# Messages kept in PSUM and taken at the start of a period

## The chip, the cores and the metric

The kernel runs on one core of a Trainium2 chip. The metric is device time in microseconds; three runs of the kernel before gave 9139.07, 9145.55 and 9146.39 us, median 9145.55.

## The reference

A message-passing layer on a graph of 12,500 nodes with 800,000 edges; D = 64, edge attributes of 16 numbers, all in fp32:

```python
N, deg, D, De = 12500, 64, 64, 16
E = N * deg
m_in = jnp.concatenate([x[src], x[dst], e_attr], axis=-1)
msg = _silu(m_in @ w_msg)                 # E x D
agg = _segment_sum(msg, dst, N)           # N x D
return _silu(jnp.concatenate([x, agg], axis=-1) @ w_upd)
```

## The kernel before

The nodes are cut into 128 buckets of 98. The product of `w_msg` is split by its rows: `A_d` holds `x @ w_msg[0:64]` for all nodes in HBM, `BW` holds for each bucket the 98 rows `x @ w_msg[64:128]` with the 16 rows for `e_attr` below them, so that one product with a one-hot of the local destination and the edge's attributes gives the rest of a message. The kernel does two things side by side, in software-pipelined *periods* written out by hand (`period`): it sorts edges into buckets, and it computes messages of edges that are sorted already.

**Sorting** (class `Step`, 1024 edges a step, 782 steps). ScalarE makes one-hots of the buckets (`onehot`: eight squares and a Relu, tile `hf`); VectorE sums them up (`sums`, tile `G`); TensorE counts (`count`, tile `z`); VectorE takes ranks (`ranks`, L418) and expands the records into slots (`expand`, tile `X`, L431); TensorE moves them to their buckets (`move`, tile `pl`, L447); ScalarE copies a chunk out (`blk`, L451) and GpSimd scatters it to the store `st` in HBM. The four stages of a step lie in successive periods. A step holds 8 tiles of 128 edges; a chunk holds 8 tiles in the first 140 steps and 12 later, so there the widths of the expansions, and of the matmuls one period behind them, go round with period three.

**Messages** (class `Batch`, 8 tiles of 128 edges, 6 in one stage). In its first period GpSimd gathers the rows of `A_d` by source index (`gather`, L629, one indirect DMA a tile, tile `g`, three buffers) and VectorE makes the one-hot `q` (L634). In the second, TensorE transposes it (`tq`), ScalarE copies it to `qt` (L646), and TensorE takes the product with the bucket's `BW` into the PSUM bank `pre` (`product`, L652). In the third, `message` adds the gathered rows to `pre` on VectorE (L658), the sum going to SBUF, and ScalarE takes the Silu (L659). Where tiles of a bucket come in units of four (`QU`), `parts` splits the fp32 message into three bf16 pieces: it reads the upper halves of the fp32 words as bf16 and subtracts, two VectorE instructions (L667). These batches are called split; all but the first stage's and the last ones are. In the fourth period TensorE reduces the pieces with the one-hot into the PSUM bank `ag` (`reduce`, L678; L680 where not split), and VectorE adds the sums to the accumulators (`add`, L691 and L693). At the end the nodes are updated from the accumulators.

**Groups.** A `Group` of 64 tiles is formed ahead of its use: `fourth` and `middle` compute from the buckets' pointers which tiles are taken. TensorE puts sums into a tile `ps` (`middle`), which VectorE reads one period later, in `fourth`: L535 and L536 in one period, L574 and L575 (`rows`) in the next. `ps` has the tag "ag", and the pool `pag` has one buffer, so `ps` and the aggregate `ag` of `reduce` use one bank in turn. The framework makes the first write of a new tile wait for all reads of the tile that had the buffer before it, wherever in the text they stand.

Every engine works through its own instructions in the order in which `period` calls the functions; semaphores come from the data. Before the change the order on VectorE is: one-hot `q`, reading of a forming group, ranks, message sum, addition of the aggregate, expansion, sums of the one-hots, placing of a chunk, two subtractions. On ScalarE: the next step's one-hot, copy of attributes, weights, copy of the transposes, Silu, copies for sums and chunks. On TensorE: count, transposes, reduction, moves, product (between the moves in every third period), sums of a forming group.

Of the kernel before, what the change touches and what calls it, by code (L numbers as in the profile page):

```python
# [14 lines left out]
P = 128  # L15
NBK = 128
BK = 98
D = 64
# [12 lines left out]
BT = 8  # L31
NBG = 8
GT = NBG * BT
QU = 4
# [12 lines left out]
def mpnn_kernel(tc, x, e_attr, src, dst, w_msg, w_upd, out):  # L47
    nc = tc.nc
# [22 lines left out]
    with es:  # L71
# [90 lines left out]
        class Nodes:  # L162
# [193 lines left out]
        mp = pool("mp", 2)  # L356
# [245 lines left out]
        class Batch:  # L602
# [50 lines left out]

            def message(t):
                w = t.n * D
                t.msg = mp.tile([P, 3, BT * D], F32, name="msg")
                u_ = t.msg[:, 2, :]
                nc.vector.tensor_tensor(out=u_[:, 0:w], in0=t.pre[:, 0:w], in1=t.g.rearrange("p a b -> p (a b)")[:, 0:w], op=OP.add)  # L658
                nc.scalar.activation(t.msg[:, 0, 0:w], u_[:, 0:w], AF.Silu)  # L659

            def parts(t):

                t.split = t.grp.u == QU
                if t.split:
                    up = t.msg.bitcast(BF16).rearrange("p k (f two) -> p k f two", two=2)
                    for k in range(2):
                        nc.vector.tensor_tensor(out=t.msg[:, k + 1, :], in0=t.msg[:, k, :], in1=up[:, k, :, 1], op=OP.subtract)  # L667

            def reduce(t):
                t.ag = pag.tile([P, 512], F32, name="ag")  # L670
                w = 3 * D
                if t.split:
                    q = t.q.bitcast(BF16).rearrange("p i (k two) -> p i k two", two=2)[:, :, 0:BK, 1]
                    m = t.msg.bitcast(BF16).rearrange("p k (f two) -> p k f two", two=2)[:, :, :, 1]
                for i in range(t.n):
                    u, k = i // t.grp.u, i % t.grp.u
                    if t.split:
                        nc.tensor.matmul(t.ag[0:BK, u * w:(u + 1) * w].rearrange("p (k d) -> p k d", d=D), q[:, i, :], m[:, :, i * D:(i + 1) * D], start=(k == 0), stop=(k == t.grp.u - 1))  # L678
                    else:
                        nc.tensor.matmul(t.ag[0:BK, u * D:(u + 1) * D], t.q[:, i, 0:BK], t.msg[:, 0, i * D:(i + 1) * D], start=(k == 0), stop=(k == t.grp.u - 1))  # L680

            def add(t):
                if t.b0 is not None:
# [14 lines left out]
        def period(step=None, batch=None, ptr_new=None):  # L698

            h, z, p, s = step, pipe["h"], pipe["z"], pipe["s"]  # L700
            q, t, a, r = batch, pipe["q"], pipe["t"], pipe["a"]
# [6 lines left out]
                s.scatter()  # L708
            if q:
                q.gather(BT // 2, BT)  # L710
            if h:
                h.onehot()
            if q:
                q.onehot()
            for g in forms:
                g.fourth()
            if z:
                z.count()
            if t:
# [2 lines left out]
                t.transpose(1)  # L722
            if r:
                r.reduce()
            if z:
                z.ranks()
            if a:
                a.message()
            if r:
                r.add()  # L730
            if z:
                z.expand()
            if h:
                h.sums()
            if p:
# [179 lines left out]
        while work["used"] < large or (work["forming"] and work["forming"][-1].k < 2):  # L915
            b = take()
# [67 lines left out]
        while work["used"] < whole or lasts or work["cur"] is not None or work["forming"]:  # L984
            b = take()
# [165 lines left out]
```

## Time and profile before

| what | value |
|---|---|
| median of three runs | 9145.55 us |
| the profiled execution's own time | 9133.99 us |
| its span, first to last instruction | 9132.2 us |
| busy: PE, PE weight loads, DVE, ACT, POOL | 8125.5, 5898.7, 8140.8, 5100.7, 6771.0 us |
| mean granted TensorE clock | 0.966 |

Busy times say how long an engine had instructions in execution. POOL's row counts only the descriptor work of its DMAs; the 0.30 us of issue between two of them is shown as idle. A row of the timeline gives start, busy time, engine, line, operation, tiles, shapes and count, and in brackets the idle time before and what ended it. A row of the groups gives busy time, mean ns of one, and idle time before.

### The profile page before, as it was taken

To read this page: it belongs to the slowest core of one execution; us is meant where nothing else is said; L and a number is where in the kernel's file an instruction comes from. 1 tells how busy PE (TensorE), PEld (TensorE's weight loads), DVE (VectorE), ACT (ScalarE), POOL (GpSimd) and SP (SyncE) were. 2 spreads that over 40 slices of the span, in tenths; PEclk is the share of its full clock that TensorE was granted. 3 is DMA by queue.
4 is the path that set the end of the run, shared out by engine and by line. 5 is a ranking of instruction groups with operands and counts; after the bars stand their busy time and mean duration, and the time that the engine had idled before them with its cause. 6 is when DMAs were issued, how large, how long until landed. Compare 5 with 4: busy or idle time off the path is not lost. (4 is left out here: it accounts for less than half of the span.)

```text
span 9132.2 us, 146484 instructions
## 1 busy us (share of the span) xinstructions
PE 8125.5 (89%) x44080; PEld 5898.7 (65%) x44842; DVE 8140.8 (89%) x17569; ACT 5100.7 (56%) x12609; POOL 6771.0 (74%) x6915
## 2 busy tenths in 40 slices
PE   8999999988888888898889898898888888888677
PEld 5677776666666666666666666666666666666676
DVE  7899999999999999999999999999999999998332
ACT  6566665555555555555555555555555555555222
POOL 1677777777777777777777777777777777777776
PEclk9999999999999999999999999999999999999666
DMA  2222222222222222222222222222222222222323
GB/s 66 55 60 62 61 60 56 50 56 50 55 54 50 55 51 55 49 56 51 55 50 54 56 51 50 54 55 50 56 51 54 50 55 55 51 54 48 58 48 50
DMA packets 650600, 492.47 MB, mean 54 GB/s; under 512 B 482887, under 2 KB 519303, under 8 KB 649799
## 3 DMA queue, kind: packets, MB, share of 16 engines
q0 software_dynamic: 238976, 349.72, 16.9%
q1 hardware_dynamic: 408119, 132.58, 6.9%
q8 instruction: 360, 5.90, 0.3%
q14 instruction: 441, 3.61, 0.1%
q10 hardware_dynamic: 2704, 0.66, 0.1%
HBM read 330.05 MB, written 152.30 MB: 53 GB/s over the span
## 5 line engine op out<-in xcount | busy, mean ns | idle before, releaser
L629 POOL DMA_INDIRECT g<-A_d,sidx x6322 | 6186.0, 978 | 1953.4 <-issue 1557.3
L447 PE MATMUL pl<-X,hf 128*128 128x223 f32 (+5 forms) x12512 | 4093.2, 478 | 0.0
L447 PEld LDWEIGHTS pl<-X,hf 128*128 128x128 f32 x12512 | 2303.0, 191 | 1263.5 <-issue 912.4
L431 DVE TENSOR_TENSOR X<-cb,rec 128x442 f32<-128x442 f32 (+5 forms) x3128 | 2647.3, 909 | 27.1
L383 ACT ACTIVATE hf<-iof,shi 128x128 f32<-128x128 f32 x6256 | 1909.4, 389 | 1056.7 <-PE pl L447 1053.2
L652 PEld LDWEIGHTS pre<-w,qt 114*128 114x128 f32 x10496 | 1289.8, 195 | 322.3 <-issue 298.5
L652 PE MATMUL pre<-w,qt 114*128 114x64 f32 x10496 | 1265.2, 275 | 44.3 <-DVE msg L658 39.9
L659 ACT ACTIVATE msg<-msg 128x512 f32<-128x512 f32 (+1 forms) x818 | 501.8, 613 | 1270.3 <-DVE msg L658 1265.5
L418 DVE TENSOR_REDUCE rank<-z 128x8 f32<-128x1024 f32 x782 | 949.6, 1214 | 66.5 <-PE z L413 64.6
L658 DVE TENSOR_TENSOR msg<-pre,g 128x512 f32<-128x512 f32 (+1 forms) x818 | 546.2, 668 | 485.7 <-DMA g<-A_d,sidx 285.5
L646 ACT ACTIVATE qt<-tq 114x1024 f32<-114x1024 f32 (+1 forms) x818 | 800.8, 979 | 312.2 <-PE tq L643 308.9
L411 PE MATMUL z<-G,onesb 128*128 128x384 bf16 x1564 | 515.8, 330 | 467.3 <-DVE G L392 416.4
L451 ACT ACTIVATE blk<-pl 128x512 f32<-128x512 f32 (+1 forms) x568 | 325.2, 573 | 1074.9 <-PE pl L447 1034.6
L667 DVE TENSOR_TENSOR msg<-msg 128x512 f32<-128x512 f32 x1312 | 903.6, 689 | 22.9
L384 ACT ACTIVATE hf<-hf,ones 128x1024 f32<-128x1024 f32 x782 | 899.1, 1150 | 25.4
L643 PE MATMUL tq<-ident,q 128*114 128x128 f32 x6322 | 887.1, 286 | 14.2 <-ACT nodes L188 12.8
L643 PEld LDWEIGHTS tq<-ident,q 128*114 128x114 f32 x6322 | 781.9, 142 | 139.8 <-ACT nodes L188 20.5
L678 PE MATMUL ag<-msg,q 128*98 128x192 bf16 x5248 | 580.0, 253 | 307.9 <-DVE rb L575 118.2
L469 POOL DMA_INDIRECT st<-blk,ptrs x567 | 566.7, 999 | 333.4 <-issue 147.8
L634 DVE TENSOR_TENSOR q<-cb,lo 128x784 f32<-128x784 f32 (+1 forms) x818 | 768.5, 939 | 0.7
L678 PEld LDWEIGHTS <-q 128*98 128x98 bf16 x5248 | 497.1, 126 | 396.6 <-issue 338.1
L411 PEld LDWEIGHTS <-onesb 128*128 128x128 bf16 x1564 | 152.7, 98 | 384.6 <-DVE G L392 281.1
(145 smaller groups left out, 6768.0 us busy)
## 6 DMA issues: line engine op xcount, KB each, us to landing
g<-A_d,sidx POOLq DMA_INDIRECT x6322
ea<-in_e_attr SPq DMA_DIRECT2D x260, 192.0 KB
rt<-st SPq DMA_DIRECT2D x1312, 34.0 KB
st<-blk,ptrs POOLq DMA_INDIRECT x567
rt<-st SPq DMA_DIRECT2D x434, 8.5 KB
nodes<-in_x SPq DMA_DIRECT2D x62, 98.0 KB
rt<-st SPq DMA_DIRECT2D x320, 17.0 KB
A_d<-nodes SPq DMA_DIRECT2D x32, 98.0 KB
```

Source lines behind the costliest of these rows:

```text
L383: nc.scalar.activation(c.hf[:, k, :], iof, AF.Square, bias=c.hi[:, k:k + 1])
L384: nc.scalar.activation(c.hf, c.hf, AF.Relu, bias=ones, scale=-1.0)
L418: nc.vector.tensor_reduce(out=c.rank, in_=c.z, axis=AX.X, op=OP.max)
L431: nc.vector.tensor_tensor(out=c.x[:, k:k + 2, 2:2 + n * R].rearrange("p k (s c) -> p k s c", c=R), in0=hit[:, k:k + 2, 0:n, None].to_broad ...
L447: nc.tensor.matmul(pl[:, 0:w], c.hf[:, k, :], c.x[:, k, 0:w], start=False, stop=(n == c.size - 1))
L629: nc.gpsimd.indirect_dma_start(out=t.g[:, i, :], out_offset=None, in_=A_d, in_offset=bass.IndirectOffsetOnAxis(ap=t.grp.sidx[:, k:k + 1], ...
L634: nc.vector.tensor_tensor(out=t.q[:, 0:n, 0:BK], in0=ioB[:, None, 0:BK].to_broadcast([P, n, BK]), in1=t.grp.lo[:, i0:i0 + n, None].to_broa ...
L643: nc.tensor.transpose(t.tq[0:KQ, j * P:(j + 1) * P], t.q[:, j, :], ident)
L646: nc.scalar.activation(t.qt[:, 0:w], t.tq[0:KQ, 0:w], AF.Copy)
L652: nc.tensor.matmul(t.pre[:, i * D:(i + 1) * D], t.qt[:, i * P:(i + 1) * P], w, start=True, stop=True)
L667: nc.vector.tensor_tensor(out=t.msg[:, k + 1, :], in0=t.msg[:, k, :], in1=up[:, k, :, 1], op=OP.subtract)
L678: nc.tensor.matmul(t.ag[0:BK, u * w:(u + 1) * w].rearrange("p (k d) -> p k d", d=D), q[:, i, :], m[:, :, i * D:(i + 1) * D], start=(k == 0 ...
```

## The change

The message sum is written back to `pre` in PSUM. In split batches the Silu works there in place, ScalarE rounds it to bf16 with a copy into a bf16 tile, VectorE subtracts that piece from `pre` in place, ScalarE rounds the rest, and VectorE subtracts once more into the third piece. In other batches the Silu goes from PSUM to an fp32 tile. In the period, the message sum becomes VectorE's first instruction and Silu and first rounding ScalarE's first; the first subtraction stands behind the one-hot `q`, the second behind the ranks. The next step's one-hot on ScalarE moves behind the copy of the transposes. The reading of a forming group (`fourth`) moves from ahead of the ranks to behind the second subtraction, and in the text behind `reduce`; the addition of the aggregate moves behind the expansion.

```diff
             def message(t):
                 w = t.n * D
-                t.msg = mp.tile([P, 3, BT * D], F32, name="msg")
-                u_ = t.msg[:, 2, :]
-                nc.vector.tensor_tensor(out=u_[:, 0:w], in0=t.pre[:, 0:w], in1=t.g.rearrange("p a b -> p (a b)")[:, 0:w], op=OP.add)
-                nc.scalar.activation(t.msg[:, 0, 0:w], u_[:, 0:w], AF.Silu)
-
-            def parts(t):
-
                 t.split = t.grp.u == QU
+                pre = t.pre[:, 0:w]
+                nc.vector.tensor_tensor(out=pre, in0=pre, in1=t.g.rearrange("p a b -> p (a b)")[:, 0:w], op=OP.add)
                 if t.split:
-                    up = t.msg.bitcast(BF16).rearrange("p k (f two) -> p k f two", two=2)
-                    for k in range(2):
-                        nc.vector.tensor_tensor(out=t.msg[:, k + 1, :], in0=t.msg[:, k, :], in1=up[:, k, :, 1], op=OP.subtract)
+                    t.msg = mp.tile([P, 3, BT * D], BF16, name="msg")
+                    nc.scalar.activation(pre, pre, AF.Silu)
+                    nc.scalar.activation(t.msg[:, 0, 0:w], pre, AF.Copy)
+                else:
+                    t.msg = mp.tile([P, BT * D], F32, name="m32")
+                    nc.scalar.activation(t.msg[:, 0:w], pre, AF.Silu)
+
+            def part(t, k):
+
+                if t.split:
+                    nc.vector.tensor_tensor(out=t.pre if k == 1 else t.msg[:, k, :], in0=t.pre, in1=t.msg[:, k - 1, :], op=OP.subtract)
+                    if k == 1:
+                        nc.scalar.activation(t.msg[:, k, :], t.pre, AF.Copy)
...
-            if h:
-                h.onehot()
+            if a:
+                a.message()
             if q:
                 q.onehot()
-            for g in forms:
-                g.fourth()
+            if a:
+                a.part(1)
             if z:
                 z.count()
...
             if r:
                 r.reduce()
+            if h:
+                h.onehot()
             if z:
                 z.ranks()
             if a:
-                a.message()
+                a.part(2)
+            for g in forms:
+                g.fourth()
+            if z:
+                z.expand()
             if r:
                 r.add()
-            if z:
-                z.expand()
...
-            if a:
-                a.parts()
             for g in forms:
                 g.middle()
```

More of the change, by code (lines that the diff above doesn't have):

```diff
@@ L677, in reduce @@
                     if t.split:
-                        nc.tensor.matmul(t.ag[0:BK, u * w:(u + 1) * w].rearrange("p (k d) -> p k d", d=D), q[:, i, :], m[:, :, i * D:(i + 1) * D], start=(k == 0), stop=(k == t.grp.u - 1))
+                        nc.tensor.matmul(t.ag[0:BK, u * w:(u + 1) * w].rearrange("p (k d) -> p k d", d=D), q[:, i, :], t.msg[:, :, i * D:(i + 1) * D], start=(k == 0), stop=(k == t.grp.u - 1))
                     else:
-                        nc.tensor.matmul(t.ag[0:BK, u * D:(u + 1) * D], t.q[:, i, 0:BK], t.msg[:, 0, i * D:(i + 1) * D], start=(k == 0), stop=(k == t.grp.u - 1))
+                        nc.tensor.matmul(t.ag[0:BK, u * D:(u + 1) * D], t.q[:, i, 0:BK], t.msg[:, i * D:(i + 1) * D], start=(k == 0), stop=(k == t.grp.u - 1))
             def add(t):
```

1 line of the change is left out of this document (removed).

## The prediction

> **What bounds the kernel now.** I read the page first, then the busy time by stages, then the groups and the waits of the even middle (2000 to 8000 us), and last the timeline of single periods.
>
> ```profile
> span 9132.2 us, 146484 instructions
> 500.00:1000.00 500.00, 495.18 (x2949) 382.71 (x3004) 473.80 (x1250) 321.92 (x805) 379.03 (x395) 1.00 0.27 62
> 4000.00:5000.00 1000.00, 896.17 (x4814) 632.65 (x4901) 943.79 (x1961) 574.96 (x1428) 763.54 (x777) 0.99 0.24 53
> 8600.00:8800.00 200.00, 155.91 (x878) 146.19 (x878) 73.22 (x217) 51.49 (x106) 151.66 (x161) 0.61 0.32 54
> ```
>
> The columns of a stage are its length and the busy time of PE, PE weight loads, DVE, ACT and POOL. There are three stages. Early (until about 1344 us, batches that are not split) PE is full: 495 of 500 us. In the middle (to about 8400 us) DVE is at 94% and POOL at 76%. At the end only POOL keeps its pace. The middle holds three quarters of the time, so I look for what it waits for.
>
> ```profile
> L629 POOL DMA_INDIRECT g<-A_d,sidx x4290 | 4226.4, 985 | 1307.3 <-issue 1046.1 <-DMA g<-A_d,sidx 174.0 <-DVE q L634 33.8
> L667 DVE TENSOR_TENSOR msg<-msg 128x512 f32<-128x512 f32 x1072 | 738.2, 689 | 18.6
> L418 DVE TENSOR_REDUCE rank<-z 128x8 f32<-128x1024 f32 x536 | 650.2, 1213 | 0.0
> L678 PE MATMUL ag<-msg,q 128*98 128x192 bf16 x4288 | 467.6, 251 | 257.0 <-DVE rb L575 97.4 <-DVE msg L667 96.4 <-DVE wl L536 61.1
> L658 DVE TENSOR_TENSOR msg<-pre,g 128x512 f32<-128x512 f32 x536 | 368.2, 687 | 173.7 <-issue 84.8 <-DMA g<-A_d,sidx 84.5
> L659 ACT ACTIVATE msg<-msg 128x512 f32<-128x512 f32 x536 | 337.3, 629 | 944.8 <-DVE msg L658 944.4
> L451 ACT ACTIVATE blk<-pl 128x512 f32<-128x512 f32 x358 | 211.9, 592 | 567.8 <-PE pl L447 567.8
> ```
>
> ```profile
> DVE msg L658 <- issue: 84.8, 126, 1.8
> DVE msg L658 <- DMA g<-A_d,sidx: 84.5, 122, 2.5
> ```
>
> The L418 row counts 536 periods in 6000 us, 11.19 us each. POOL never rests in them: 985 ns of gather and about 0.30 us of issue, over and over. DVE has one stall, ahead of the message sum (L658): 173.7 us, in 126 + 122 = 248 waits. DVE instructions that do not wait start about 0.08 us before the one ahead ends, so a wait costs that as well: 173.7 + 248 x 0.08 = 194 us, or 0.36 us per period. So the gathers set the pace, and DVE by itself would need 11.19 - 0.36 = 10.83 us. DVE and POOL are nearly even, and whichever the change makes longer decides.
>
> One period in which a forming group is read back shows the rest:
>
> ```profile
> 5777.99 1.41 DVE L667 TENSOR_TENSOR msg<-msg 128x512 f32<-128x512 f32 x2
> 5779.32 0.97 DVE L634 TENSOR_TENSOR q<-cb,lo 128x784 f32<-128x784 f32 x1
> 5780.20 0.15 DVE L574 SCALAR_TENSOR_TENSOR row<-ps,iof 1x16 int32<-1x16 f32 x1
> 5780.29 0.15 DVE L575 CAST rb<-ps 1x16 int32<-1x16 f32 x1
> 5780.37 1.20 DVE L418 TENSOR_REDUCE rank<-z 128x8 f32<-128x1024 f32 x1
> 5780.50 0.85 PE L678 MATMUL ag<-msg,q 128*98 128x192 bf16 x8 [1.50 <-DVE rb L575]
> 5780.92 1.00 ACT L646 ACTIVATE qt<-tq 114x1024 f32<-114x1024 f32 x1
> 5781.18 6.03 PE L447 MATMUL pl<-X,hf 128*128 128x359 f32 x16
> 5781.78 0.69 DVE L658 TENSOR_TENSOR msg<-pre,g 128x512 f32<-128x512 f32 x1 [0.21 <-DMA g<-A_d,sidx]
> 5782.39 0.55 DVE L691 TENSOR_REDUCE sum<-ag 98x128 f32<-98x384 f32 x1
> 5782.51 0.63 ACT L659 ACTIVATE msg<-msg 128x512 f32<-128x512 f32 x1 [0.59 <-DVE msg L658]
> 5783.37 0.17 DVE L427 TENSOR_TENSOR X<-rank,limc 128x8 f32<-128x8 f32 x1
> 5786.82 0.45 DVE L392 TENSOR_TENSOR G<-hf 128x256 bf16<-128x256 f32 x1
> 5787.05 1.90 PE L652 MATMUL pre<-w,qt 114*128 114x64 f32 x16
> 5787.75 2.44 ACT L383 ACTIVATE hf<-iof,shi 128x128 f32<-128x128 f32 x8
> 5788.30 1.41 DVE L667 TENSOR_TENSOR msg<-msg 128x512 f32<-128x512 f32 x2
> 5790.21 1.15 ACT L384 ACTIVATE hf<-hf,ones 128x1024 f32<-128x1024 f32 x1
> ```
>
> The product (L652), whose result the next message sum needs, ends at 5788.95, after the two roundings (L667) of 5788.30 have begun. That is harmless today, because the message sum comes 3.8 us behind the period's first L667.
>
> **Part 1, a new wait on DVE in every split period.** Call m the start of the message sum, now the first DVE instruction of a period. Behind it comes the one-hot (L634), 0.61 us later (5781.78 to 5782.39 is how long a message sum holds DVE). The first subtraction would follow 0.89 us after that (5779.32 to 5780.20 plus rounding), at m + 1.49. But it now needs two ScalarE instructions, the Silu and the first rounding, one after the other. ACT starts 0.04 us after the sum's end (5782.47 to 5782.51). Neither a Silu on PSUM nor a rounding copy is in the trace. The nearest rows are the Silu in SBUF, 629 ns, and the copy out of PSUM of the same shape, 592 ns. For the rounding I take 592, for the Silu 600, as it reads PSUM like the copy, with 550 to 630 as bounds; 0.03 us for each handover. So it starts at m + 0.69 + 0.03 + 0.60 + 0.03 + 0.59 + 0.03 = m + 1.97, and DVE stands still for 0.48 us. Queued behind it on DVE are ranks, expansion and everything else. The second rounding copy (0.59) is hidden by ranks (1.13 us, 5780.37 to about 5781.5, if nothing is waited for). One thing is saved: today the second L667 waits for the first and the pair takes 1.33 us (5777.99 to 5779.32); apart they take 2 x 0.61. Net +0.48 - 0.11 = +0.37 us per period.
>
> **Part 2, the operands move to PSUM.** In the trace a tensor_tensor with a PSUM input takes 687 ns (L658), one with both in SBUF 689 (L667), so I cost this at nothing for DVE. The Trainium skill (VectorE: DVE Perf Modes, section "The TRN2 errata") gives 120 cycles fixed for PSUM-sourced and 58 for SBUF-sourced VectorE instructions; by that, at the page's 0.96 GHz, two subtractions would be dearer by 0.13 us per period, an estimate of +82 us in all. The two rows here show no such difference.
>
> For POOL the move counts:
>
> ```profile
> 5778.88 1.34 POOL L629 DMA_INDIRECT g<-A_d,sidx  x1 [0.30 <-issue]
> 5781.77 0.94 POOL L629 DMA_INDIRECT g<-A_d,sidx  x1 [0.30 <-issue]
> ```
>
> The instructions of L536, one for each group that forms, from 500 to 1344 us and from 1344 to 8400 us:
>
> ```profile
> L536 DVE TENSOR_SCALAR wl<-ps x24: 146/146/150, 504.1 to 1316.0; 128x1 f32<-128x1 f32 x24
> L536 DVE TENSOR_SCALAR wl<-ps x79: 146/148/151, 1378.8 to 8383.6; 128x1 f32<-128x1 f32 x79
> ```
>
> Beside the L667 pair a gather takes 1.34 us, beside the message sum 0.94. The mean of 985 ns holds (985 - 944) x 4290 = 176 us of such stretching, 0.33 us per period; most of it goes, and POOL would need about 10.9 us. DVE then needs 10.83 + 0.37 = 11.20 us and becomes the bound: the gather waits go (-0.36), the new wait comes (+0.37). A group of 64 tiles makes 8 batches and 79 groups fall into the middle, so 632 periods: -228 + 234 = +6 us.
>
> **Part 3, the reading of a forming group moves behind the second subtraction.** The group's sums ("ps") and the aggregate ("ag") share one PSUM bank, a pool with one buffer. So PE's reduction (L678) must wait until DVE has read the sums: L536 in one period of a group, L575 in the next. Today it waits for that too (1.50 us in the quoted period), but the reading stands right behind the one-hot. After the change it stands behind message, one-hot, subtraction, ranks, subtraction: m + 1.97 + 0.61 + 1.13 + 0.61 = m + 4.32, done at m + 4.56, and L678 starts at m + 4.61. In the quoted period, with m = 5777.99, that is 5782.60 and not 5780.50: 2.10 us later. Queued behind L678 on PE are the 16 matmuls of L447 and the product, so the product ends at 5788.95 + 2.10 = 5791.05. DVE alone would be ready for the next message sum at 5782.48 (reading done) + 4.93 (L427 to the next L667) + 0.98 (the addition, L691 to L427) = 5788.39. It now waits for the product: 2.7 us, and as DVE is the bound, all of it is lost. In the groups whose second reading falls in such a period (short expansion, long L447 matmuls; I count 44 of 79 by following L574 through the timeline) that costs 44 x 2.7 = 119 us. In the other 35 the product comes early in the second period and PE is late into the period after it. I have no single row for that: bounds are 0 and 2.7 per group, I take the middle, 1.4, or 49 us. Together +168 us.
>
> **Part 4, the early stage.**
>
> ```profile
> 768.53 1.45 PE L652 MATMUL pre<-BW,qt 114*128 x12
> 769.66 0.76 DVE L634 TENSOR_TENSOR q<-cb,lo 128x588 f32<-128x588 f32 x1
> 771.47 1.00 PE L680 MATMUL ag<-msg,q 128*98 128x64 f32 x10
> 772.15 0.55 DVE L658 TENSOR_TENSOR msg<-pre,g 128x384 f32<-128x384 f32 x1
> ```
>
> PE runs without a gap here and the reduction (L680) starts 1.49 us after the product's end (769.98). With the message sum first, DVE starts it at 770.03, then one-hot (770.50), ranks (771.18), reading (772.31), read at 772.53: L680 would start at about 772.58 in a reading period, 1.1 us later. 24 groups have 48 such periods, PE is the bound, so +53 us; bounds are 0 and, with one more microsecond of ranks, 100.
>
> **Part 5, what is hidden.** The one-hot of the next step moves behind the transposes' copy on ACT. Its squares and Relu (2.44 + 1.15, about 3.5 us with overlap) then follow copy (until m + 3.29), weights and the 1.00 us of L646 and end at about m + 8.0. DVE needs them at L392, which in the quoted period would come at m + 4.49 + 3.45 + 0.98 = m + 8.9. Margin 0.9 us: hidden, and if that cover fails, each 0.1 us of lateness is 63 us. At the end POOL sets the pace and no length changes, but with DVE as the bound POOL may enter that stage with up to two batches more done (16 x 1.25 = 20 us): I take -10.
>
> **The sum.** +6 + 168 + 53 - 10 = +217 us on the profiled execution, which took 9134.0 us (1.8 more than its span); the median of the three runs, 9145.55, is 11.6 above that. On the median: 9360 us, +2.4%. The measurement of this kernel can tell a difference of about 0.2% (18 us).
>
> **The rivals.** *A, the gathers win: faster.* If what bounds is the gather queue and the roundings cost DVE little, the period falls to POOL's 10.9 us, 0.3 x 632 = about -190, so near 8955 us, or 9010 with the early loss. The Trainium skill (SBUF — State Buffer, section "Who interferes with whom") says that a VectorE instruction with two SBUF inputs contends with a GpSimd instruction that reads SBUF, and one with a single SBUF input does not; the 1.34 and 0.94 us rows agree. For it: the stretched gathers. Against it: DVE would have to come out below 10.9 us, so the new stall would have to be under about 0.18 us and not 0.48, and the readings would have to be hidden. Chance 0.08. *B, the bank costs nothing: about the same.* If the readings' lateness is absorbed, +6 - 10 and some of the early loss are left: 9140 to 9190, say 9155. For it: PE has 10% idle time in the middle. Against it: in the quoted period nothing idle stands between the reduction's start and the product's end (5780.50, 5781.18, 5787.05, 5788.95). Chance 0.12. *C, tighter coupling in ordinary periods too: slower still.* The message sum now meets the product's end, and ACT's chain of 8.0 us meets the sums' start, in every period. At 0.3 us per period: +190 more, 9550. For it: in the quoted period the product ends after the period's end even now. Against: the new stall of 0.48 delays DVE, not PE, which widens that margin. Chance 0.08.
>
> **How the numbers follow.** The forecast has 0.72, with its own range from 9290 (35 groups at nothing, short Silu) to 9450 (all groups at 2.7, early loss 100). Leaving out A and part of C, and taking in most of B, the range is 9160 to 9450. Faster: A and a sliver of B, 0.10. Same: 0.05, the part of B near 9146. Slower: 0.85.
>
> **What would show it.** Right: the first subtraction waits for ACT by 0.4 to 0.5 us in every split period; the gather waits at the message sum vanish, and in their place stand waits for the product of over 2 us, some 44 of them; gathers mean under 0.96 us; L678 waits for L536 and L575 by about 3 us. Wrong: POOL still without pause in the middle (A), no product waits (B), L392 waiting for L384 (C).

## The result, and the profile after

The changed kernel takes 9648.03 us (median of four runs, 9644.43 to 9651.14) against 9142.36 us for the kernel before on the same chip: ratio 1.0554, 95% interval 1.0538 to 1.0570. The direction was forecast (slower, 0.85), the size was not: +506 us where the sum gave +217, outside the range (9450).

The page's first line:

```profile
span 9646.1 us, 147735 instructions
```

The three stretches that were shown of before, with the same columns (length; busy PE, weight loads, DVE, ACT, POOL; granted clock; DMA share; GB/s):

```profile
500.00:1000.00 500.00, 463.53 (x2672) 353.62 (x2723) 430.94 (x1141) 305.45 (x732) 344.16 (x355) 0.98 0.21 55
4000.00:5000.00 1000.00, 884.43 (x4561) 621.72 (x4645) 895.88 (x1838) 650.97 (x1520) 705.12 (x734) 0.95 0.19 50
8600.00:8800.00 200.00, 176.62 (x904) 123.51 (x920) 180.00 (x368) 130.69 (x305) 140.99 (x147) 0.95 0.19 49
```

No engine is full any more: PE falls from 495 to 464 of 500 us in the early stage, DVE from 944 to 896 and POOL from 764 to 705 of 1000 us in the middle (the last row now still lies in the middle). The granted TensorE clock falls from 0.99 to 0.95. Set side by side by the first split addition and the last ranks, the early stage ends 113 us later (1348 to 1461), the 633 periods of the middle take 7495 us instead of 7071 (11.84 a period against 11.17), and the rest is 24 us shorter: +514 us of span.

Groups of the middle (2000 to 8000 us): busy time, mean ns of one, and idle time before with what ended it.

```profile
L629 POOL DMA_INDIRECT g<-A_d,sidx x4049 | 3871.8, 956 | 1237.7 <-issue 1038.8 <-DMA g<-A_d,sidx 115.0 <-DVE cb L428 39.6
L447 PE MATMUL pl<-X,hf 128*128 128x359 f32 (+5 forms) x8101 | 2956.5, 519 | 0.0
L682 PE MATMUL ag<-msg,q 128*98 128x192 bf16 x4056 | 431.8, 251 | 293.7 <-DVE wl L536 173.0 <-DVE rb L575 120.7
L670 DVE TENSOR_TENSOR pre<-pre,msg 128x512 f32<-128x512 f32 x506 | 354.1, 700 | 204.6 <-ACT msg L662 204.6
L658 DVE TENSOR_TENSOR pre<-pre,g 128x512 f32<-128x512 f32 x506 | 354.0, 700 | 167.2 <-PE pre L652 135.7 <-issue 14.3 <-DMA st<-blk,ptrs 3.7
L469 POOL DMA_INDIRECT st<-blk,ptrs x337 | 344.7, 1023 | 546.9 <-ACT blk L451 509.3 <-issue 37.6
L662 ACT ACTIVATE msg<-pre 128x512 bf16<-128x512 f32 x506 | 302.3, 597 | 15.9
L444 PE MATMUL pl<-done,onesb 1*128 1x512 bf16 x337 | 135.4, 402 | 229.3 <-ACT blk L451 229.3
L464 DVE SCALAR_TENSOR_TENSOR LOST<-blk 128x1 f32<-128x1 f32 x337 | 52.1, 155 | 102.4 <-ACT blk L451 101.7
```

The forecast wait is there: L670 stands 0.40 us for the first rounding (L662) in each of 506 periods, 0.48 with the lost overlap. The gathers are down to 956 ns, and their waits ahead of the message (L658) are gone, but the message now waits for the product. Three rows were not forecast: the first matmul of a new chunk (L444), the placing of a chunk (L464) and the scatter (L469) all wait for the chunk's copy `blk` on ScalarE.

A period in which a forming group is read; only some of its rows are shown:

```profile
5029.33 0.70 DVE L658 TENSOR_TENSOR pre<-pre,g 128x512 f32<-128x512 f32 x1 [0.18 <-issue]
5031.30 0.70 DVE L670 TENSOR_TENSOR pre<-pre,msg 128x512 f32<-128x512 f32 x1 [0.40 <-ACT msg L662]
...
5033.04 0.68 DVE L670 TENSOR_TENSOR msg<-pre,msg 128x512 bf16<-128x512 f32 x1
5033.71 0.15 DVE L536 TENSOR_SCALAR wl<-ps 128x1 f32<-128x1 f32 x1
5033.90 1.44 PE L682 MATMUL ag<-msg,q 128*98 128x192 bf16 x8 [3.54 <-DVE wl L536]
5035.81 6.84 PE L447 MATMUL pl<-X,hf 128*128 128x223 f32 x16
5042.49 1.90 PE L652 MATMUL pre<-w,qt 114*128 114x64 f32 x16
5044.42 0.70 DVE L658 TENSOR_TENSOR pre<-pre,g 128x512 f32<-128x512 f32 x1 [3.44 <-PE pre L652]
```

Two stretches of the same period, for TensorE alone (length, PE busy, granted clock):

```profile
5031.00:5035.00 4.00, 1.09 (x8) 0.82 0.15 34
5035.00:5039.00 4.00, 4.00 (x12) 0.50 0.11 25
```

TensorE stands 3.54 us for the reading, then runs reduction, moves and product, and VectorE stands 3.44 us for the product: 15.1 us from message to message. The stretches show its clock: 0.82 in the one with the pause, 0.50 in the next.

Every period of the middle can be sorted by what it does, from one batch's one-hot to the next (474 ordinary ones; 79 that read `ps` for L536, "first"; 79 that read it for L575, "second"). Mean length in us:

| kernel | ordinary | first reading | second reading |
|---|---|---|---|
| before | 11.04 | 11.84 | 11.28 |
| after | 11.51 | 12.80 | 12.92 |

So the middle's +425 us are 474 x 0.47 = 223 in ordinary periods and 79 x (0.96 + 1.64) = 206 in reading periods. In the early stage the 59 reading periods are longer by 1.82 (30) and 1.76 us (29), which is 106 of its 113 us.

### The profile page after: what moved, and what is told of

It reads as the page before. It is cut to its first block, busy times and chain, and to the rows that moved or that the text cites. A ratio compares the mean times of both kernels' runs of the same rounds, so it can differ in the third digit from the quotient of the medians.

```text
span 9646.1 us, 147735 instructions
## 1 busy us (share of the span) xinstructions
PE 8445.0 (88%) x44080; PEld 6090.6 (63%) x44842; DVE 8179.4 (85%) x17569; ACT 5947.6 (62%) x13921; POOL 6638.8 (69%) x6915
## 5 line engine op out<-in xcount | busy, mean ns | idle before, releaser
L629 POOL DMA_INDIRECT g<-A_d,sidx x6322 | 6045.0, 956 | 2045.1 <-issue 1624.7
L447 PE MATMUL pl<-X,hf 128*128 128x223 f32 (+5 forms) x12512 | 4413.1, 507 | 0.0
L447 PEld LDWEIGHTS pl<-X,hf 128*128 128x128 f32 x12512 | 2478.8, 205 | 1674.8 <-issue 1277.2
L661 ACT ACTIVATE pre<-pre 128x512 f32<-128x512 f32 x656 | 381.9, 582 | 1787.6 <-DVE pre L658 1787.6
L469 POOL DMA_INDIRECT st<-blk,ptrs x567 | 575.8, 1015 | 889.5 <-ACT blk L451 672.0
L658 DVE TENSOR_TENSOR pre<-pre,g 128x512 f32<-128x512 f32 (+1 forms) x818 | 557.5, 682 | 446.5 <-PE pre L652 200.4
L384 ACT ACTIVATE hf<-hf,ones 128x1024 f32<-128x1024 f32 x782 | 898.2, 1149 | 25.4
L670 DVE TENSOR_TENSOR pre<-pre,msg 128x512 f32<-128x512 f32 x656 | 459.0, 700 | 277.0 <-ACT msg L662 276.5
L672 ACT ACTIVATE msg<-pre 128x512 bf16<-128x512 f32 x656 | 391.8, 597 | 372.3 <-DVE pre L670 372.3
```

What stands on the lines that cost most here:

```text
L384: nc.scalar.activation(c.hf, c.hf, AF.Relu, bias=ones, scale=-1.0)
L447: nc.tensor.matmul(pl[:, 0:w], c.hf[:, k, :], c.x[:, k, 0:w], start=False, stop=(n == c.size - 1))
L469: i = nc.gpsimd.indirect_dma_start(out=st, out_offset=bass.IndirectOffsetOnAxis(ap=c.ptr, axis=0), in_=c.blk[:, 2:], in_offset=None)
L629: nc.gpsimd.indirect_dma_start(out=t.g[:, i, :], out_offset=None, in_=A_d, in_offset=bass.IndirectOffsetOnAxis(ap=t.grp.sidx[:, k:k + 1], ...
```

## The experiments

All times are medians; the ratio is to the kernel before on the same chip.

| run | what it is | us | ratio, 95% interval |
|---|---|---|---|
| a1 | after, reading early | 9383.17 | 1.0265 (1.0247 to 1.0282) |
| a2 | after, one-hot first | 10180.63 | 1.1136 (1.1118 to 1.1155) |
| a3 | both | 9327.47 | 1.0203 (1.0186 to 1.0220) |
| a5 | after, TensorE kept at work (transposes into a new buffer) | 10032.15 | 1.0973 (1.0955 to 1.0992) |
| a6 | after, the same into the bank `ag` | 9896.85 | 1.0838 (1.0820 to 1.0856) |
| a7 | a1, twelve of them into the bank `ag` | 9542.02 | 1.0448 (1.0431 to 1.0465) |
| a9 | a1, the twelve into the tile `tq` | 9185.37 | 1.0062 (1.0045 to 1.0079) |
| a10 | after, the twelve into `tq`, sixteen into the bank `ag` | 9638.15 | 1.0560 (1.0542 to 1.0577) |
| b1 | after's data, before's order | 9255.36 | 1.0137 (1.0120 to 1.0154) |
| b2 | before, reading late | 9274.99 | 1.0158 (1.0141 to 1.0175) |
| b4 | before, message first | 9149.51 | 1.0021 (1.0011 to 1.0031) |
| c4 | a1, ranks ahead of the subtraction | 9128.49 | 1.0000 (0.9990 to 1.0009) |
| c5 | c4, second subtraction later | 9023.16 | 0.9885 (0.9868 to 0.9901) |
| c6 | c5, early message in its old place | 8989.89 | 0.9849 (0.9833 to 0.9866) |

### Undoing the two moves: a1, a2, a3

```diff
 a1:             if q:
                     q.onehot()
+                for g in forms:
+                    g.fourth()
                 if a:
                     a.part(1)
 a2:        +    if h:
+                    h.onehot()
                 if a:
                     a.message()
```

> The changed kernel with the reading of the forming group (fourth) put back right behind the batch's one-hot, ahead of reduce. Three theories for the +506 us. READING: fourth behind reduce holds the one bank ag, TensorE stands 2 to 3.5 us in each reading period (127 waits of ag in 6,000 us, against 105 waits of pl for the chunk copy), and this is most of the loss: its share by count of waits is 127 of 232 of the middle's +425 us, 233 us, and half to all of the early stage's +113; so about 9300 to 9360 us, the waits of ag for wl and rb gone. CHUNK COPY: the copy of pl queued on ScalarE behind the moved one-hot is the loss: 9580 us or more, waits of ag gone and nothing won. COUPLING: the message first, with ScalarE between its sum and its first subtraction, costs by itself: 9600 us or more.

> The changed kernel with only the step's one-hot (eight Squares and a Relu on ScalarE) put back to the front of the period, ahead of the message. CHUNK COPY: the waits of pl and of LOST for the copy go, 105 of 232 waits of the middle, so 190 us of its +425, less up to 150 us for a Silu that stands behind the one-hot (ScalarE waited 3.4 us before a Silu in the one period looked at, and the one-hot takes 3.6): 9460 to 9610 us. READING: 9640 us or more, since the bank is held as before. COUPLING: later than 9650, by the longer wait of the first subtraction (0.3 us in each of 762 periods, some 9800).

> The changed kernel with both moved back: the reading ahead of reduce, the step's one-hot at the front. READING and CHUNK COPY together: the two savings add, 9648 - 300 - 190 + 150 = about 9150 to 9310 us, near the kernel before, and TensorE has hardly a pause over 2 us and few stretches at half clock. COUPLING: 9550 us or more; what is left above 9142 then belongs to the message-first order.

Measured: a1 wins 265 us, 23 us short of READING's range (9300 to 9360) and far from the other two: the waits of `ag` fall to 28 us. a2 lies far above CHUNK COPY's range and above the 9800 of COUPLING, and separates no two theories: TensorE's waits for the chunk's copy go, but with the late reading kept, the one-hot in front is 530 us worse than after. Its Squares wait for a buffer that the late moves free, the Silu stands behind them, and the first subtraction waits up to 5.5 us for it (577 us in 6,000). a3 is 56 us better than a1, and misses its 9150 to 9310 by 17 us. Groups of a1:

```profile
L682 PE MATMUL ag<-msg,q 128*98 128x192 bf16 x4160 | 428.6, 246 | 28.1 <-DVE wl L536 14.5 <-DVE rb L575 13.4
L658 DVE TENSOR_TENSOR pre<-pre,g 128x512 f32<-128x512 f32 x520 | 363.7, 699 | 130.6 <-PE pre L652 91.9 <-issue 15.6 <-DMA st<-blk,ptrs 4.6
L447 PE MATMUL pl<-X,hf 128*128 128x461 f32 (+5 forms) x8312 | 2998.6, 515 | 0.0
L444 PE MATMUL pl<-done,onesb 1*128 1x512 bf16 x346 | 140.2, 405 | 349.4 <-ACT blk L451 349.4
L464 DVE SCALAR_TENSOR_TENSOR LOST<-blk 128x1 f32<-128x1 f32 x346 | 53.5, 155 | 64.2 <-ACT blk L451 64.0
```

Rows of a1's timeline, where a chunk closes and the next opens:

```profile
5020.85 1.90 PE L652 MATMUL pre<-w,qt 114*128 114x64 f32 x16
5022.63 1.15 ACT L384 ACTIVATE hf<-hf,ones 128x1024 f32<-128x1024 f32 x1
5024.14 0.58 ACT L451 ACTIVATE blk<-pl 128x512 f32<-128x512 f32 x1
5024.77 0.58 PE L444 MATMUL pl<-done,onesb 1*128 1x512 bf16 x1 [2.02 <-ACT blk L451]
5025.28 3.79 PE L447 MATMUL pl<-X,hf 128*128 128x223 f32 x8
```

With the reading out of the way, the second cause stands alone. In every third period a chunk closes ahead of the product and the next opens behind it. The copy `blk` now queues on ScalarE behind the moved one-hot (its Relu, L384, ends at 5023.78, and one short copy stands between), TensorE pauses 2.02 us, and the eight matmuls behind the pause take 3.79 us. The same eight behind a pause of 0.47 us in the kernel after:

```profile
5015.85 2.00 PE L447 MATMUL pl<-X,hf 128*128 128x223 f32 x8
```

In the kernel before, the first matmul of a chunk waits for nothing. Its group in the middle:

```profile
L444 PE MATMUL pl<-done,onesb 1*128 1x512 bf16 x357 | 137.5, 385 | 0.0
```

a3 shows that the moved one-hot makes this pause. Over all such places between 2000 and 8000 us, the next chunk opens straight behind the product in the kernel before and in a3, and 2.02 us behind it in a1 (means); the eight matmuls that follow take 2.00, 2.01 and 3.24 us. With the pause, VectorE's waits for the copy (64.0 us in a1, 0.9 in a3) and for the product (91.9 and 1.9) go too. What a3 gains by this it loses in part at the first subtraction: with the Silu behind the one-hot on ScalarE, its wait grows from 144.0 to 263.9 us.

### Is it the pause or the clock behind it: a5, a6, a7, then a9, a10

TensorE repeats transposes of the batch where it stood, so that it stays at work; nothing is moved. a5 writes them to a new buffer of the pool of `tq`, a6 and a7 to free columns of the bank `ag`, a9 and a10 the twelve to `tq` itself and a10 the sixteen to free columns of `ps`. (a5 repeats sixteen at both places; the lines below are those of the other four, with the tile written to left out where it is not `ps`.)

```diff
+            for g in forms:
+                if t and g.b0 is None and g.k in (1, 2):
+                    t.warm(16, g.ps)      # a6, a10: ahead of reduce
             if r:
                 r.reduce()
 ...
+            if t and r and p and p.turn == 1:
+                t.warm(12)                # a7, a9: this one alone
             if p:
                 p.move(1)
```

> The changed kernel in its own order; in periods in which a forming group reads, and in those in which a chunk opens behind the product, TensorE repeats the batch's eight transposes twice into the other buffer of that tile (about 2.1 us at full clock), so that it works where it stood. Nothing else is moved; the repeated values are not used. CLOCK: the pauses cost mostly by the half clock that follows (809 us at half rate in the middle, 217 stretches of 3.4 us): the stretches fall below 60, TensorE gets back up to 1.7 us for each, and the time to 9300 to 9450 us. PAUSE: the wait itself is what is lost, or VectorE sets the pace whatever the clock: 9640 to 9750 us, though the stretches at half clock go.

> The changed kernel in its own order, with transposes of the batch repeated on TensorE into columns of the bank ag that nobody reads: 16 (2.1 us) ahead of reduce in the periods in which a forming group's answer is read, 12 (1.6 us) ahead of the second move in the periods in which a chunk opens behind the product. It replaces a5, whose repeated transposes had to wait for ScalarE's copy of the one tile they share with tq. Nothing is moved; the repeated values are not used. CLOCK: the half clock behind the pauses lengthens the later products of the same period, so that the message and LOST wait: TensorE's product of the chunks falls from 5.68 back to 5.25 us a period, the stretches at half clock from 217 in the middle to below 60, and the time to about 9400 to 9500 us (up to 0.25 us in each of 633 periods and half of the early stage's 72 us). PAUSE: what is lost is the waiting itself, and VectorE's waits stay at 1.25 us a period: 9620 us or more, though the half clock goes.

> a1 (reading early) with the 12 repeated transposes ahead of the second move in the periods in which a chunk opens behind the product; there TensorE stood 173 times for 2.0 us in a1 and ran 208 stretches at half clock in the middle. CLOCK: stretches below 40, products of the chunks 5.25 instead of 5.61 us a period, 9383 down to 9230 to 9310 us. PAUSE: 9370 us or more.

These three told little: the added work fell behind waits of its own. In a5 the other buffer did not exist (the tile fills both banks of its pool), so the transposes waited 268 us for ScalarE's copy; in a6 and a7 the twelve waited 239 and 369 us for VectorE's read of the bank `ag`. The pauses stayed and work was added behind them, and so the times are no verdict on either theory. In a7 the transposes took 0.69 us a period, and the period grew by 0.26 us.

> The kernel of a8 once more, since on that chip every kernel, the one before too (11834 us), stood in waits that no work of the program ends. The expectations are the same. CLOCK: products of the chunks 5.61 down to about 5.25 us a period, 9270 to 9330 us. PAUSE: the half clock costs nothing by itself: 9365 us or more.

> a6 again with its 12 repeated transposes of the second pause written to the tile tq, as in a9, so that both sets fall into the pauses: the changed kernel in its own order, late reading and all, only with TensorE at work where it stood. In a9 that took 198 us from a1 and VectorE's waits for the copy and for the product with them. CLOCK: most of the price of the late reading is the half clock too: products of the chunks 5.68 down to about 5.25 us a period, 9648 down to 9250 to 9400 us. PAUSE: the late reading costs by the time that TensorE stands, which the added work doesn't shorten, and only a9's part comes back: 9430 to 9500 us.

Here they fell into the pauses. Groups of a9:

```profile
L447 PE MATMUL pl<-X,hf 128*128 128x359 f32 (+5 forms) x8544 | 2862.7, 485 | 0.0
L663 DVE TENSOR_TENSOR pre<-pre,g 128x512 f32<-128x512 f32 x535 | 374.4, 700 | 71.6 <-issue 26.6 <-DMA g<-A_d,sidx 20.1 <-PE pre L657 6.5
L444 PE MATMUL pl<-done,onesb 1*128 1x512 bf16 x356 | 135.2, 380 | 91.8 <-ACT blk L451 90.7
L464 DVE SCALAR_TENSOR_TENSOR LOST<-blk 128x1 f32<-128x1 f32 x356 | 54.2, 152 | 0.0
```

CLOCK, and by more than it forecast: with 12 useless transposes in every third period a9 is 198 us *faster* than a1 (2.0% by the ratios, or 185 us, since the two ran on different chips). The stretches at half clock (granted clock 0.50) fall from 208 to 63 in the middle, a matmul of L447 from 515 to 485 ns, VectorE no longer waits for the chunk's copy, and its wait for the product goes from 91.9 to 6.5 us. The chunk still opens late, 1.81 us behind the product against 2.02 in a1, but the eight matmuls behind it take 2.00 us instead of 3.24. Nothing else was made earlier, so the gain is the half clock's but for what those 0.2 us are worth.

```profile
L447 PE MATMUL pl<-X,hf 128*128 128x223 f32 (+2 forms) x8160 | 2750.2, 487 | 0.0
L688 PE MATMUL ag<-msg,q 128*98 128x192 bf16 x4080 | 427.4, 248 | 101.2 <-DVE wl L536 73.6 <-DVE rb L575 27.6
L469 POOL DMA_INDIRECT st<-blk,ptrs x339 | 353.2, 1042 | 506.4 <-ACT blk L451 465.2 <-issue 40.9 <-DMA g<-A_d,sidx 0.3
```

In a10, the changed kernel's own order, the clock comes back as well (L447 at 487 ns, 56 stretches instead of 217), and the time hardly moves: it misses even PAUSE's range (9430 to 9500). So the two causes do not add up:

| ratio to before | TensorE pauses | TensorE kept at work |
|---|---|---|
| reading late (as changed) | 1.0554 | 1.0560 |
| reading early | 1.0265 | 1.0062 |

The late reading costs 2.9% beside the half clock and 5.0% without it. As long as it sets the pace in the reading periods (12.85 and 13.14 us in a10, 12.80 and 12.92 in after), a faster TensorE behind it wins only in the ordinary ones (11.36 against 11.51). A part of that gain is lost to a wait that a10 adds: VectorE's reading waits for the transposes in the bank that they share, 0.38 us in a second reading period and 1.29 in one of the early stage, some 80 us in all with the first ones (an estimate from these means). So a10 bounds what the clock is worth there at about 90 us; it does not give it exactly.

### Each part in the kernel before: b2, b4, and b1

```diff
 b2 (before):            if a:
                             a.message()
+                        for g in forms:
+                            g.fourth()
 b4 (before):    +       if a:
+                            a.message()
                         if q:
                             q.onehot()
 b1 (after): message behind ranks; then add, the expansion's two
             small steps, part(1), its first product, part(2), the rest
```

> The kernel before with one step moved: the reading of the forming group stands behind the ranks and the message, so behind reduce on TensorE too. LATENESS alone: the same price as between the changed kernel and a1, 265 us, so about 9400 us, with waits of ag for wl and rb of 2 to 3.5 us and half clock behind them. LATENESS ONLY WITH THE MESSAGE FIRST: TensorE makes up for the pause before anyone waits for it, since here the message is read 3 to 4 us into the next period: 9142 to 9230 us, though the pauses and the half clock are there.

> The kernel of b3 once more, for the reason given with a9: the kernel before with its message's sum and Silu at the front. The expectations: 9142 to 9300 us if the early message only waits for the product instead of its gathers; 9142 us within 40 if nothing but the tight pair of message and subtraction costs; 9300 us or more, with waits for the DMA of g, if the gathers come late for it.

> The change's data without its order: the message stays in PSUM and ScalarE does Silu and the two roundings, but the order is that of the kernel before (one-hots and reading at the front, message behind the ranks), and the subtractions stand among the expansion: the first behind its two small steps and the second behind its first product. VectorE has the same 10.57 us of work a period. COUPLING: the loss of a1 against the kernel before (0.37 us a period) is the wait of the first subtraction right behind its message (0.28) and of the copy of the chunk, so with work between them VectorE's idle time falls below the 0.62 us of before, and gathers are no more stretched by a subtraction with two inputs in SBUF: 10.8 to 11.0 us a period, 8900 to 9050 us. If the PSUM form itself costs (ScalarE full, one bank for message and product): 9250 us or more.

b2, groups of the middle:

```profile
L629 POOL DMA_INDIRECT g<-A_d,sidx x4314 | 4205.1, 975 | 1315.2 <-issue 1032.5 <-DMA g<-A_d,sidx 214.2 <-DVE G L392 9.8
L678 PE MATMUL ag<-msg,q 128*98 128x192 bf16 x4312 | 480.6, 254 | 356.6 <-DVE wl L536 182.3 <-DVE rb L575 102.2 <-DVE msg L667 71.9
L658 DVE TENSOR_TENSOR msg<-pre,g 128x512 f32<-128x512 f32 x539 | 367.2, 681 | 0.0
L469 POOL DMA_INDIRECT st<-blk,ptrs x360 | 366.6, 1018 | 114.8 <-issue 83.2 <-ACT blk L451 6.0 <-ACT G L390 5.2
```

b2 lies between its two cases (9142 to 9230, about 9400). The pauses are about as long as in after (182.3 and 102.2 us), and reading periods grow, to 12.38 and 12.93 us, but the middle is 7047 us, not longer than before's 7071: ordinary periods shrink from 11.04 to 10.63. The POOL rows say why. Ahead of each gather stand 0.305 us of idle time (1315.2 / 4314) and ahead of each scatter 0.32 (114.8 / 360), hardly more than the issue gap that stands ahead of every gather in the kernel before (1307.3 / 4290 = 0.305): GpSimd works without pause, and what VectorE loses in one period it makes up in the next, since it no longer waits for gathers there. In after, 1.62 us stand ahead of each scatter (546.9 / 337), most of it for the chunk's copy. The early stage, where TensorE is full (495 of 500 us), pays: 1528 us against 1348. b4 falls where its first two cases overlap and does not part them; it shows that the message in front, alone, costs 0.2%. b1 missed COUPLING's range: 9255 instead of 8900 to 9050. It falls into the second case, by which the PSUM form itself would cost (9250 or more); c6 below, with the same form, shows that it need not. In b1 the subtractions lie at the wrong places for the other engines. In 6,000 us TensorE's product waits 193.2 us for the second one, and the first waits 245.3 us for the rounding, which stands behind the transposes' copy in ScalarE's order.

### A chip on which all was slow: a8, b3, c1, c2

> a7 again with its 12 repeated transposes written to the tile tq itself, which ScalarE has copied by then: in a7 they went to columns of ag and stood there 369 us behind VectorE's read of that bank, so the pause stayed and 0.69 us a period of work came behind it (11.54 to 11.80 us a period, 0.37 us for each us that TensorE got more to do). Here they fall into the pause of 2.0 us and only keep TensorE at work. CLOCK: products of the chunks 5.61 down to about 5.25 us a period, and by the 0.37 of a7 that is worth 0.13 us a period, 85 us: 9270 to 9330 us. PAUSE: the half clock costs nothing by itself: 9365 us or more.

> The kernel before with one step moved: the message's sum and Silu at the front of the period, ahead of the batch's one-hot; message in SBUF, both subtractions at the end, reading where it was. COUPLING by the early message alone: VectorE waits ahead of it for the product, 0.25 us a period as in a1, beside what it waits for now (0.31, which was for gathers), so 9142 to 9300 us; and since the subtractions stand far behind, a1's 0.28 is not there. If the tight pair message and subtraction is all of a1's loss: 9142 us within 40. A message that comes 4 us sooner also asks for its gathers 4 us sooner: if these are then late, 9300 us or more with waits for the DMA of g.

> a1 (reading early) with the step's Relu and its sums behind the first move: ScalarE then does the eight Squares, the chunk's copy, the Relu, so the copy waits 1.6 us less. CHUNK COPY: the waits of pl for blk (349 us in 6,000) and of LOST (0.126 us a period) go, with them the stretches at half clock behind them, and part of VectorE's wait ahead of the message (0.253): 11.54 down to 11.2 to 11.35 us a period, 9170 to 9270 us. COUPLING: the first subtraction's 0.28 stays and the sums now wait for the Relu: 9350 us or more.

> c1 with the ranks ahead of the first subtraction, and the two small steps of the expansion ahead of the second, so that VectorE has 1.1 us of work while ScalarE does Silu and the first rounding. COUPLING: the first subtraction's wait of 0.28 us a period goes: c1 less 100 to 180 us, about 9030 to 9130 us, thus at or below the kernel before. If the wait only changes its place (the ranks come 0.7 us sooner and wait for the counts of TensorE, or the product waits for the second subtraction in the one bank pre): c1 within 40 us.

On the chip of these four the kernel before took 11834 us, and the runs 11674, 11258, 11535 and 11738; all engines stood in waits that the profile ends with "issue" or "remote", thus with no work of the program (737.7 us of VectorE's message in a8). All four came out 0.9 to 4.9% below that, a8 and b3 too, while the same kernels lie above the kernel before elsewhere (a9, b4). No time of them is compared with the others. Two waits inside the program were plain enough to mend: in c1 the sums stood 0.46 us a period for the Relu, in c2 the second subtraction 2.5 us for a rounding queued behind the Squares.

### Putting it right: c4, c5, c6

```diff
 c4 (a1):   message, q.onehot, fourth, count, transposes, reduce
-                a.part(1); h.onehot(); z.ranks(); a.part(2)
+                z.ranks(); a.part(1); h.onehot()   # Relu and sums behind
+                z.expand(part=0); a.part(2)        # move(0) in turn 1
 c5 (c4):   +    z.expand(part=1)                   # first product
                 a.part(2)
 c6 (c5):   message behind the ranks where a.grp.u != QU
```

> a1 (reading early) with two more steps undone. The Relu and the sums of the step stand behind the first move only in the periods in which a chunk opens behind the product (in c1 they did so in all, and VectorE's sums waited 0.46 us a period for them), so that the copy of the chunk waits for the Squares alone. The ranks and the two small steps of the expansion stand between message, first and second subtraction (1.1 and 0.57 us of VectorE's work), and the Squares behind the first subtraction's rounding on ScalarE (in c2 they stood ahead of it and the second subtraction waited 2.5 us). COUPLING and CHUNK COPY together are a1's loss against before (0.37 us a period): their waits, 0.28 and 0.13 us, and part of the 0.25 ahead of the message go: 11.54 down to 11.0 to 11.2 us a period, 9030 to 9170 us. If the waits only change their place (ranks for the counts, product for the second subtraction): 9300 us or more.

> c4 with the second subtraction behind the first product of the expansion (0.84 us of VectorE's work more ahead of it). COUPLING: in c4 its wait for the second rounding, 0.284 us a period, is the largest that is left on VectorE; it goes, in 633 periods 180 us: 8940 to 9000 us, ahead of both kernels. If the product then waits for that subtraction in the one bank pre (9 us in 6,000 in c4, 193 in b1): 9050 us or more.

> c5 with the message behind the ranks, its old place, in those periods alone whose batch isn't split (the early stage and the last batches), where no subtraction follows. VectorE's wait ahead of the message was 0.199 us a period there in c4, 0.038 in the kernel before, and the early stage 36 us longer: c5 less 20 to 40 us. If the early stage is set by the copy of the chunk (0.124 us against 0.039): c5 within 10 us.

c4 is level with the kernel before, within its forecast: first subtraction and chunk copy cost nothing any more, and one wait is left on VectorE, 0.284 us a period.

```profile
L681 DVE TENSOR_TENSOR msg<-pre,msg 128x512 bf16<-128x512 f32 x538 | 372.3, 692 | 152.7 <-ACT msg L683 152.7
```

c5 takes it away and wins 105 us, not the 180 that it would be worth by VectorE alone, so it lies between its two cases (the product's wait for that subtraction grows from 9.4 to 44.8 us); c6 wins 33 more and is the fastest of all, 1.5% below the kernel before. Groups of c6:

```profile
L642 POOL DMA_INDIRECT g<-A_d,sidx x4376 | 4190.9, 958 | 1333.6 <-issue 987.3 <-DMA g<-A_d,sidx 230.4 <-DVE ACC L710 52.7
L671 DVE TENSOR_TENSOR pre<-pre,g 128x512 f32<-128x512 f32 x547 | 382.8, 700 | 105.2 <-DMA g<-A_d,sidx 42.3 <-issue 19.6 <-PE z L416 12.5
L683 DVE TENSOR_TENSOR msg<-pre,msg 128x512 bf16<-128x512 f32 x548 | 373.0, 681 | 0.0
L482 POOL DMA_INDIRECT st<-blk,ptrs x364 | 364.5, 1002 | 110.9 <-issue 51.2 <-ACT qt L659 27.7 <-ACT w L635 16.8
```

Ahead of each gather and each scatter stand 0.305 us (1333.6 / 4376 and 110.9 / 364): GpSimd is full again, at 10.95 us a period instead of 11.17. The difference is the gather's 958 ns instead of 985, eight times: 0.22 us in 633 periods, 137 us. That is all that the change had to win in the middle, and c6 has it: 6930 us against 7071.

## Why the prediction was right and where it failed

**Part 1 held.** L670 waits 0.40 us, or 0.48 with the overlap, in the split periods of the middle, and starts 1.98 us behind the message, where 1.97 was worked out: Silu 582 ns on PSUM (600 taken), rounding 597 (592 taken). By parts 1 and 2 an ordinary period was to grow by 0.01 us; free of the two causes below, in a9, it grows by 0.11 (11.04 to 11.15). Of the waits ahead of the message, which were to vanish, 0.11 us a period are left there.

**Part 2 held.** Subtractions on PSUM take 681 to 700 ns against 689, so the prediction's estimate of 82 us for a dearer PSUM operand is not borne out. The gathers fall to 956 ns, and where nothing else is late GpSimd's floor is 10.95 us (10.9 forecast).

**Part 3 held in size, not in its place.** Reading periods cost 206 us in the middle, against 168. The bank and the 16 matmuls and product behind it are as described; a1 shows the cause by taking it away. But the wait was foreseen at the message, over 2 us some 44 times. It stands there only 10 times; in second readings most of it is at the placing of the chunk (L464, 1.06 us of idle time in each), which waits for the same late matmuls through the copy and comes earlier in VectorE's order.

**Part 4 was sized too low:** 106 us in reading periods, not 53. It was 59 periods instead of 48, as six groups form ahead of 500 us, and 1.8 us each instead of 1.1, again at L464 (1.31 to 1.55 us).

**Part 5 is the step that failed.** It followed the moved one-hot to its next reader on VectorE and called it hidden, with 0.9 us of margin. That margin held; but ScalarE's queue holds one more instruction behind it, the chunk's copy, and on that wait TensorE's next chunk, VectorE's placing and GpSimd's scatter. Behind the pause of 2 us, half clock then adds 1.2 us to the next eight matmuls (3.24 against 2.00 in a1), and the message waits for the product (0.22 us in an ordinary period). Ordinary periods were to stay within 0.01 us and are 0.47 longer, 223 us in all, the largest error of the sum. Of the 0.47, the early reading takes 0.08 away (11.43 in a1) and the clock kept up another 0.28 (11.15 in a9). In a3, with the one-hot back in front, the pause itself is gone. What is queued behind the moved instruction was looked up for VectorE and not for ScalarE. (At the end the time behind the last ranks falls by 24 us, against 10 assumed.)

**The rivals.** C, tighter coupling in ordinary periods at 0.3 us, came nearest in time (9550) with 0.08, and its first half is seen, a message that waits for the product. Its second, L392 waiting for L384, is not: the link was the copy, not the sums. A, the gathers win, is what c6 does, with the waits gone by another order: 8990, where A gave 8955 to 9010. For the change as it stands A did not come true.

## What to carry to other kernels

When an instruction moves back in an in-order queue, list everything between its old and its new place *and* everything now behind it, on its own engine first; a copy that frees a bank is the one to look for. Find out which engine has no pause at all (here GpSimd, with 0.305 us of issue ahead of each DMA and no other idle time): another's wait can cost nothing as long as that stays true, as in the middle of b2, and is felt once it fails, as in after. That busy and idle time of its rows add up to the whole stretch says nothing, as they do in every kernel; look at the idle time of each instruction. A step split over two engines needs other work between its halves: c4 to c6 keep the change's data, change the order alone, and turn +5.5% into 0.0, -1.2 and -1.5%.

## What the runs showed of the hardware

A pause of TensorE of 2 us was enough here for half the clock: 2.02 us in a1, then 3.79 us for eight matmuls that took 2.00 otherwise. In a1's middle there are 164 pauses over 2 us, none over 3, and 208 stretches at half clock, most of 3.41 us; in a9 none over 2 us, and 63 stretches. The Trainium skill (TensorE: Matmul & The Clock Gate, section "Part 1: The HAM clock gate (the "warmup" mystery)") has the half rate begin after at least one idle window of about 3.4 us, and says that the window runs freely. The length of the stretches agrees; that it takes 3.4 us of idling does not, for here shorter pauses did it again and again. The length of the pause alone does not decide, though. Between 2000 and 8000 us, half clock began during or within 3.5 us behind 132 of a1's 134 pauses over 2 us and 52 of b1's 61 pauses of 1.5 to 1.8 us, but only 1 of the 76 pauses of 1.5 to 1.8 us in the kernel before; b1 has no pause over 2 us and 106 stretches. What else decides is not shown. Useless work in such a pause was worth 2.0% in a1, and nothing in after, where another wait set the pace.
